# One tuned fp32 kernel: where the first set product is drained, how the z additions are grouped, and a new hand-written order of a unit

## The chip, the core and the metric

The kernel runs on one core of a Trainium2 chip. The metric is device time in microseconds (us) of one execution, the median of several runs; lower is better. Five engines of the core work side by side, each in the order of its own queue: TensorE (PE; its weight loads are listed as PEld), VectorE (DVE), ScalarE (ACT), GpSimd (POOL) and the queue SP, which issues DMAs. Semaphores set who waits for whom.

## What is computed

Attention through 32 packed queries, then a mixture of 8 experts with a balanced gate, then a two-layer network, all in float32:

```python
p_packed = sm_attn(p, k, v)                  # 4 batches, 8 heads, 576 tokens, 64 wide
x = sm_attn(q, p_packed, p_packed)           # reshaped to 2304 tokens x 512
P = exp(x @ w_gate - max), then 8 rounds of row and column scaling
for e in range(8):                           # 512 -> 1024 -> 512
    out += P[:, e:e + 1] * (np.maximum(x @ w1[e], 0.0) @ w2[e])
r = np.maximum(out @ w_in, 0.0)              # 512 -> 2048
result = (s * (r * r) + b) @ w_out           # 2048 -> 512
```

## The kernel before

Products in float32 precision are made from high and low parts: a number is cast to a short form (high), the rest is its low part, and a product is three matmuls (`PASSES`: high x high, high x low, low x high). So every operand needs a cast (ACT) and a subtraction (POOL, or DVE where it comes from PSUM).

The mixture is cut into 32 units (`U1`) of 256 hidden columns. Each unit has four rows, one for each batch b of 576 tokens. Units 5 to 30 run in `slotw` by an order written out by hand, the strings `STEADY[0]` to `STEADY[3]`; unit 4 and the last unit run by `PLAIN`. A string lists tokens, and each token issues the instructions of one step. Each engine keeps that order for its own instructions.

The tokens of a row, for x @ w1 (`mm1w`): seven products m1 to m7 with 288 columns each, a seven-product scheme for a 2 x 2 split. m1 fills bank a; n1 (ACT, L732) copies it into bank b as a seed; m2 adds to b, m6 to a; n2, n3 (ACT, L735) are snapshots of a between m6, m5 and m3; m7 and m4 fill bank e; +b, +c, +e (DVE, L738) add snapshots; rb, rc, ra, re are the ReLU and high part (ACT, L717), lb, lc, la, le the low part (DVE, L721). There are four PSUM banks for these (tag "h").

For h @ w2: t is a tile of 128 tokens x 512 columns, six matmuls (`tile2`, L791), and te its drain by DVE (L813), weighted by the gate, into the sum `acc`. Of each of rows 0, 1 and 2, two tiles are made by seven products p1 to p7 of 256 columns instead (`set7`, L684), one row later, with two of the four "y" PSUM banks, a and b/e. u6, u5, d2, d7, d4, d3 are DVE additions of a bank into `acc` (L690); d3 is put off to the next row's token x. Product 1 belongs to two sums: before, kb (ACT, L702) copies it from bank a into a half of bank b, where p2 adds to it. `bits` and `written` keep which half of a bank has been written. s3 and S (DVE, L646) form sums of h, hs splits them (ACT L666, POOL L667) for p6, p5, p3 and p7 of the next row.

Steps for the unit as a whole: w1a, w1b split W1 (`w1_split`); zh makes z = packed values x W1 (24 matmuls, L555) into all four y banks; zo0, zo1 copy it out (ACT, L565) and send it to DRAM (SP, L567); home brings it back in another layout by four DMAs (SP, L573); za adds (`z_add`, POOL, L587) and zs splits (`z_split`, ACT L594, POOL L595) the left operands of one row; wl loads W2 (SP, L152), w2s splits it, ta adds its quarters (`t_add`, L162) and ts splits the sums (`t_split`); w1l loads the next W1 (SP, L135). hs, cv: one step of the conversion of the last network's weights (from unit 9 on, in each row), which loads and sends by SP (L174, L208). The z tiles share three buffers, the W2, stage and conversion loads two ("raw").

In `steady(u, b)` a step's token belongs to one row: its table is indexed by b. So a step can move within its row alone.

Of the kernel before, what the change touches and what calls it, by code (L numbers as in the profile page):

```python
# [9 lines left out]
F32 = mybir.dt.float32  # L10
# [30 lines left out]
W0 = UE  # L41
# [3 lines left out]
def by7(u, b):  # L45
    return W0 < u < U1 - 1 and b in SEVEN
# [3 lines left out]
def tile_kernel(ctx: ExitStack, tc: tile.TileContext, qT, kT, vv, pb, w1c, w2c, wcat64, wg, sv, bv, out):  # L50
# [107 lines left out]
    def t_add(u):  # L158

        b11, b12, b21, b22 = (raw2[u][:, 256 * n:256 * n + 256] for n in range(4))  # L160
        for to, x_, y_ in ((b11, b12, b11), (b12, b22, b12), (b22, b22, b11), (b21, b21, b22)):
            G.tensor_tensor(out=to, in0=x_, in1=y_, op=ALU.subtract)  # L162
# [19 lines left out]
    def raw_ops(key, q):  # L182

        v, half, f = key
        lo, hi, m = raw_parts(raws[key], q)
        ex = stay[0][:, :256].bitcast(U32) if stay else wt_p[-1].tile([128, 256], U32, tag="ex", name="ex")
        o = slice(512 * half + 256 * q, 512 * half + 256 * q + 256)
# [360 lines left out]
    def z_heads(u):  # L548

        z_ps[:] = [[(psa("y", "ps_z"), written(1))[0] for _ in range(2)] for _ in range(2)]  # L550
# [27 lines left out]
    def z_add(u, b):  # L578

        src = zplain[0][:, b]  # L580
        two = stay[0][:, 256:].rearrange("p (n m) -> p n m", n=2)
        one = wt_p[-1].tile([128, 1, 128], F32, tag="sums", name="sums")
        for to, x_, y_, op in ((two[:, 0], src[:, 0], src[:, 2], ALU.add),
                               (two[:, 1], two[:, 0], src[:, 1], ALU.subtract),
                               (one[:, 0], src[:, 1], src[:, 0], ALU.subtract),
                               (src[:, 0], src[:, 3], two[:, 1], ALU.subtract)):
            G.tensor_tensor(out=to, in0=x_, in1=y_, op=op)  # L587
        z_sums[u, b] = [(slice(0, 4), src), (slice(4, 6), two), (slice(6, 7), one)]

# [79 lines left out]
    def set7(u, b):  # L669
# [34 lines left out]
        jobs = {"p1": p1, "kb": kb, "p7": lambda: product(7, p["e"], True)}  # L704
        for n, to in ((2, "b"), (6, "a"), (5, "a"), (3, "a"), (4, "e")):
# [303 lines left out]
    def slot1(u, pr, q, side=()):  # L1009
# [8 lines left out]
    STEADY = {  # L1018
# [4 lines left out]
    }  # L1023
# [70 lines left out]
    with tc.tile_pool(name="ppf", bufs=1) as ppf_p, tc.tile_pool(name="w1p", bufs=2) as w1_, ExitStack() as whole, ExitStack() as start:  # L1094
# [159 lines left out]
        share(whole, y=4, h=4)  # L1254
        turns["y"] = 0
        wt = whole.enter_context(tc.tile_pool(name="wt", bufs=1))
# [10 lines left out]

        def steady(u, b):

            jobs = ({"zs": (z_split, u, 1), "w1a": (w1_split, u + 1, 0), "w1b": (w1_split, u + 1, 1),  # L1270
                     "za": (z_add, u, 2), "ta": (t_add, u), "ts": (t_split, u)},
                    {"zs": (z_split, u, 2), "zh": (z_heads, u + 1), "zo0": (z_out, 0), "zo1": (z_out, 1),
                     "za": (z_add, u, 3), "zs3": (z_split, u, 3)},
                    {"home": (z_home, u + 1), "wl": (w2_load, u + 1), "za": (z_add, u + 1, 0)},
                    {"zs": (z_split, u + 1, 0), "za": (z_add, u + 1, 1), "w2s": (w2_split, u + 1)})[b]
            if b == 3 and u + 2 < U1:
                jobs["w1l"] = load_w1, u + 2
            if by7(u, b - 1) and b:
                jobs["hs"] = h_split, b - 1
            if u > U1 // 4:  # L1280
                jobs["cv"] = next, units, None
            return jobs

        with tc.manual_schedule():
# [5 lines left out]
                     (1, 2): [(z_add, W0, 0)],  # L1290
                     (1, 3): [(z_split, W0, 0), (z_add, W0, 1)]}
            for u, pr, q in order[cut:]:
                no_gate[:] = [True] * ((pr, q) == (1, 0))
                slot1(u, pr, q, [lambda f=f, a=a: f(*a) for f, *a in first[pr, q]])
            for u in range(W0, U1):
                for b in range(B):
# [20 lines left out]
                    if u == W0:  # L1317
                        if b == 2:
                            at("1", x_split, 3)
                        for place, what in {0: {"1": "w1a", "2": "w1b"}, 1: {"1.5": "zh zo0", "1": "zo1"},  # L1320
                                            2: {"0": "home wl", "3": "za"},
                                            3: {"1.5": "zs", "2": "w1l", "3.5": "za", "4": "w2s"}}[b].items():
                            for token in what.split():
                                at(place, *steady(u, b)[token])
                    elif not last:
                        for token, job in steady(u, b).items():
                            at(token, *job)
                        if u == U1 - 2 and b == 3:
                            at("w2s", plain_home)
                    slotw(u, b, side)  # L1330
# [107 lines left out]
```

## Time and profile before

| | us |
|---|---|
| median of 3 runs | 1715.35 (1714.13 to 1718.73) |
| the profiled execution | 1717.97 |
| its span, first to last instruction | 1716.1 |
| busy in the span: TensorE | 1674.1 (98%) |
| VectorE | 1243.5 (72%) |
| GpSimd | 1137.6 (66%) |
| ScalarE | 981.4 (57%) |

Busy time of matmuls overlaps, since they are pipelined: a 288-column product is shown with some 0.56 us but the next one starts 0.40 us after it. Distances from start to start tell what TensorE spends. A profile's line for an instruction gives its start, its length, its engine and line, output<-inputs, and in brackets the idle time of the engine before it and what ended that.

### The profile page before, as it was taken

To read this page: it belongs to the slowest core of one execution; us is meant where nothing else is said; L and a number is where in the kernel's file an instruction comes from. 1 tells how busy PE (TensorE), PEld (TensorE's weight loads), DVE (VectorE), ACT (ScalarE), POOL (GpSimd) and SP (SyncE) were. 2 spreads that over 40 slices of the span, in tenths; PEclk is the share of its full clock that TensorE was granted. 3 is DMA by queue.
4 is the path that set the end of the run, shared out by engine and by line. 5 is a ranking of instruction groups with operands and counts; after the bars stand their busy time and mean duration, and the time that the engine had idled before them with its cause. 6 is when DMAs were issued, how large, how long until landed. Compare 5 with 4: busy or idle time off the path is not lost.

```text
span 1716.1 us, 29985 instructions
## 1 busy us (share of the span) xinstructions
PE 1674.1 (98%) x10777; PEld 1473.9 (86%) x10777; DVE 1243.5 (72%) x2766; ACT 981.4 (57%) x2320; POOL 1137.6 (66%) x1390
## 2 busy tenths in 40 slices
PE   6999999999999999999999999999999999999999
PEld 4678888888888888888888888888888999999998
DVE  5656656777778777777777778777776878777763
ACT  3443365655665555655565556655655666666664
POOL 0332377888888777888888778888862855555552
PEclk9999999999999999999999999999999999999999
DMA  9610014223232433232233333222320111111102
GB/s 259 172 26 19 7 41 107 75 74 87 74 102 74 103 85 103 74 90 75 77 99 90 88 96 106 75 74 75 91 82 13 37 38 37 50 38 50 39 23 110
DMA packets 62180, 130.39 MB, mean 76 GB/s; under 512 B 5968, under 2 KB 28496, under 8 KB 62032
## 3 DMA queue, kind: packets, MB, share of 16 engines
q1 hardware_dynamic: 62032, 128.49, 27.0%
q8 instruction: 84, 1.38, 0.3%
q14 instruction: 64, 0.52, 0.1%
HBM read 94.39 MB, written 34.08 MB: 75 GB/s over the span
## 4 chain that ended last, share of the span: by engine, by line
PE 62%; ACT 10%; POOL 9%; DMA 9%; DVE 5%; SPq 2%; issue 2%; POOLq 0%; ACTq 0%; DVEq 0%
PE ps L791 31%; PE ps L838 9%; DMA zp<-far 8%; PE ps_a L629 5%; POOL zz L595 5%; ACT zz L594 3%; PE ps_e L629 3%; PE ps L773 2%; PE ps_a L684 2%; PE ps_b L684 2%; SPq L573 2%; PE ps_z L555 2%; ACT stage L565 2%; ACT h L717 2%; POOL ppf L587 2%
## 5 line engine op out<-in xcount | busy, mean ns | idle before, releaser
L791 PE MATMUL ps<-w,h 128*128 128x512 f32 x3360 | 849.8, 394 | 2.1 <-DVE acc L809 0.7
L791 PEld LDWEIGHTS ps<-w,h 128*128 128x128 f32 x3360 | 606.9, 188 | 114.5 <-issue 2.6
L813 DVE SCALAR_TENSOR_TENSOR acc<-ps,pm,acc 128x512 f32<-128x512 f32 x348 | 258.7, 746 | 164.8 <-PE ps L791 164.2
L717 ACT ACTIVATE h<-ps_b 128x288 fp32r<-128x288 f32 x224 | 93.0, 415 | 149.3 <-DVE ps_b L738 70.6
L595 POOL TENSOR_TENSOR zz<-zp,zz 128x512 fp32r<-128x512 f32 x112 | 146.5, 1308 | 41.4 <-ACT zz L594 38.5
L830 POOL TENSOR_TENSOR h<-gt,h 128x384 fp32r<-128x384 f32 x64 | 65.7, 1027 | 120.2 <-ACT h L829 110.8
L735 ACT COPY snap<-ps_a 128x288 f32<-128x288 f32 x232 | 93.5, 403 | 90.3 <-PE ps_a L629 89.2
L629 PE MATMUL ps_a<-xt,zz 128*128 128x288 f32 x672 | 131.6, 304 | 13.2 <-ACT snap L735 12.9
L952 DVE TENSOR_TENSOR acc<-ps,acc 128x512 f32<-128x512 f32 x126 | 86.1, 687 | 80.3 <-PE ps L791 79.9
L629 PEld LDWEIGHTS ps_a<-xt,zz 128*128 128x128 f32 x672 | 103.3, 188 | 34.2 <-ACT snap L735 25.5
L587 POOL TENSOR_TENSOR ppf<-zp 128x128 f32<-128x128 f32 x112 | 51.6, 461 | 113.6 <-DMA zp<-far 113.6
L629 PE MATMUL ps_e<-xt,zz 128*128 128x288 f32 x672 | 126.3, 296 | 0.0
L629 PE MATMUL ps_a<-xa,zz 128*128 128x288 f32 x672 | 126.1, 296 | 0.0
L690 DVE SCALAR_TENSOR_TENSOR acc<-ps_a,pm,acc 128x256 f32<-128x256 f32 x234 | 112.2, 479 | 11.4 <-PE ps_a L684 7.9
L667 POOL TENSOR_TENSOR xa<-hp,xa 128x512 fp32r<-128x512 f32 x78 | 101.1, 1297 | 27.9 <-ACT xa L666 27.9
L721 DVE SCALAR_TENSOR_TENSOR h<-ps_b,h 128x288 fp32r<-128x288 f32 x224 | 100.9, 450 | 24.6 <-ACT h L717 24.5
L690 DVE SCALAR_TENSOR_TENSOR acc<-ps_b,pm,acc 128x256 f32<-128x256 f32 x234 | 109.5, 478 | 5.7 <-PE ps_b L684 5.6
L629 PEld LDWEIGHTS ps_a<-xa,zz 128*128 128x128 f32 x672 | 105.1, 188 | 7.7 <-ACT snap L735 0.3
L838 PE MATMUL ps<-xa,w 128*128 128x384 f32 x432 | 110.4, 336 | 0.0
L838 PE MATMUL ps<-xt,w 128*128 128x384 f32 x432 | 110.1, 335 | 0.0
L629 PEld LDWEIGHTS ps_e<-xt,zz 128*128 128x128 f32 x672 | 104.1, 189 | 4.6
L717 ACT ACTIVATE h<-ps_a 128x288 fp32r<-128x288 f32 x112 | 46.1, 411 | 89.6 <-PE ps_a L629 66.1
(298 smaller groups left out, 3620.0 us busy)
## 6 DMA issues: line engine op xcount, KB each, us to landing
far<-stage SPq DMA_DIRECT2D x54, 512.0 KB, 2.9
zp<-far SPq DMA_DIRECT2D x108, 256.0 KB, 4.6
raw<-w2c SPq DMA_DIRECT2D x32, 512.0 KB, 6.6
raw<-wcat SPq DMA_DIRECT2D x32, 512.0 KB, 3.6
acc<-kT SPq DMA_DIRECT2D x8, 576.0 KB, 9.2
out<-acc SPq DMA_DIRECT2D x18, 256.0 KB, 2.0
acc<-vv SPq DMA_DIRECT2D x5, 576.0 KB, 10.4
conv<-ppf SPq DMA_DIRECT2D x8, 128.0 KB, 4.2
```

What stands on the lines that cost most here:

```text
L587: G.tensor_tensor(out=to, in0=x_, in1=y_, op=op)
L595: G.tensor_tensor(out=zz[:, 1, o], in0=s_, in1=zz[:, 0, o].bitcast(F32), op=ALU.subtract)
L629: mmul(p_[:, :HB], zq_[u, b][:, a, LEFT[n], :], x_, start=start and m == 0, stop=m == 2, skip_group_check=True)
L667: G.tensor_tensor(out=lo, in0=from_, in1=hi.bitcast(F32), op=ALU.subtract)
L690: V.scalar_tensor_tensor(out=a, in0=p[bank], scalar=pm[:, T, e_:e_ + 1], in1=a, op0=ALU.mult, op1=ALU.add)
L717: A.activation(out=h_at(b, f, t)[0], in_=p_[:, :HB], func=AF.Relu)
L721: V.scalar_tensor_tensor(out=hl, in0=p_[:, :HB], scalar=0.0, in1=hh.bitcast(F32), op0=ALU.max, op1=ALU.subtract)
L735: A.copy(s_[n], p["a"][:, :HB])
L791: mmul(y, h[:, f, a, hc:hc + 128], ws[f][k], start=(n == 0), stop=(n == 3 * UF - 1))
L813: V.scalar_tensor_tensor(out=a, in0=y, scalar=pm[:, T, u // UE:u // UE + 1], in1=a, op0=ALU.mult, op1=ALU.add)
L838: mmul(p, w[:, a, c * 128:(c + 1) * 128], x_get(k, c, b), start=(n == 0), stop=(n == 3 * NC - 1))
L952: V.tensor_tensor(out=a, in0=y, in1=a, op=ALU.add)
```

## The change

Product 1 of a set stays in bank a and is added to `acc` by DVE (new token d1) before p6 overwrites it; p2 starts bank b by itself (token p2 takes the bank), and kb, `bits`, `written` and `turns` go.

`z_add(u, b)` adds for rows b and b + 1 in one instruction each: four of 2 x 128 elements in place of eight of 128. It is called for b = 0 and b = 2 (za0, za2). Its sums use all 512 columns of the tile `stay`, so the conversion's scratch tile `ex` moves to a tile of its own. `t_add` makes two of its four subtractions as one.

`steady(u)` is one table for all rows, so that a step can stand in any row of a unit, and all four strings are new: among others, zs3 moves from the end of row 1 to the top of row 2, home and wl swap (wl first) and move to the middle and the end of row 2, za stands in row 2 and row 0 alone, zs0 moves behind p5 of row 3, w2s from row 3 to row 2, zh ahead of n1.

```diff
     def z_add(u, b):
-        src = zplain[0][:, b]
-        two = stay[0][:, 256:].rearrange("p (n m) -> p n m", n=2)
-        one = wt_p[-1].tile([128, 1, 128], F32, tag="sums", name="sums")
+        src = zplain[0][:, b:b + 2]
+        two = stay[0].rearrange("p (b n m) -> p b n m", b=2, n=2)
+        one = wt_p[-1].tile([128, 2, 1, 128], F32, tag="sums", name="sums")
...
-        for to, x_, y_ in ((b11, b12, b11), (b12, b22, b12), (b22, b22, b11), (b21, b21, b22)):
+        for to, x_, y_ in ((left_, up, left_), (b22, b22, b11), (b21, b21, b22)):
...
-        def kb():
-            side = min(bits[turns["y"] % 4])
+        def p2():
             b_ = psa("y", "ps_b2")
-            p["b"], p["e"] = (b_[:, 256 * s:256 * s + 256] for s in (side, 1 - side))
-            written(1 - side)
-            A.copy(p["b"], p["a"])
+            p["b"], p["e"] = b_[:, :256], b_[:, 256:]
+            product(2, p["b"], True)
...
-        for k, t, d, bank in (("u6", 1, 0, "a"), ("u5", 1, 1, "a"), ("d2", 0, 0, "b"), ("d7", 1, 1, "e"),
+        for k, t, d, bank in (("d1", 0, 0, "a"), ("u6", 1, 0, "a"), ("u5", 1, 1, "a"), ("d2", 0, 0, "b"), ("d7", 1, 1, "e"),
...
     STEADY = {
-        0: "m1 m7 zs n1 ta t te m2 m6 rb n2 t m5 x lb t w1a n3 m3 te +c s3 S m4 w1b te +e ra cv rc t ts za t te te x lc re le la",
-        1: "m1 x n1 zh zo0 m6 zo1 hs m2 n2 p1 t m7 kb rb p2 te p6 zs p7 lb u6 m5 d2 p5 n3 t +c m4 u5 s3 d7 te rc +e m3 ra p3 d3 re lc le za p4 zs3 la S cv d4",
-        2: "m1 n1 x p1 t m2 m6 rb n2 m7 t home m5 hs kb te te lb p2 p6 cv u6 n3 p7 +c t d7 rc p5 m3 d2 lc m4 u5 ra za +e s3 p4 p3 S d4 re le wl d3 te la",
-        3: "m1 n1 p1 m2 x m6 hs zs rb n2 t kb m5 lb p6 te m7 p2 u6 n3 p7 +c p5 m4 d2 rc t lc za w2s +e d7 m3 u5 te re p4 ra d4 le p3 d3 w1l cv la",
+        0: "m1 n1 t m2 ta m6 w1a x t rb lb n2 te te zs1 m5 cv w1b t te x t m7 n3 +c ts te s3 t m4 m3 rc za2 te +e ra lc re le S la",
+        1: "m1 zh n1 m6 cv m7 m2 zo0 hs n2 p1 zo1 m5 rb n3 x t lb p2 d1 +c zs2 p6 p7 rc m4 u6 d2 d7 m3 p5 +e t p4 te u5 ra s3 re p3 le d4 d3 lc S te la",
+        2: "zs3 m7 t m1 n1 te t m6 hs te n2 p1 m2 rb m5 n3 x wl d1 p2 w2s p6 lb p7 +c m3 m4 u6 d7 +e p5 s3 t u5 re rc ra p3 home p4 d3 S la lc za0 d4 te le d2",
+        3: "m1 cv m7 p1 n1 x m6 m2 hs d1 n2 end p2 m5 n3 t rb lb p6 p7 cv m3 +c m4 u6 d7 p5 +e zs0 re ra u5 p4 d4 rc te le t p3 w1l d2 te d3 lc la",
     }
```

## Rows read from the trace of the kernel before

**Rows 1.** The page's busy line of the whole span: busy us, share, instructions.

```profile
PE 1674.1 (98%) x10777; PEld 1473.9 (86%) x10777; DVE 1243.5 (72%) x2766; ACT 981.4 (57%) x2320; POOL 1137.6 (66%) x1390
```

**Rows 2.** Windows: length, busy by engine, clock: stretch, two units, a piece.

```profile
239.46:1239.02 999.56, 981.89 (x6278) 875.63 (x6277) 762.52 (x1765) 589.28 (x1477) 796.93 (x1010) 1.00 0.32 87
...
469.25:507.29 38.04, 37.72 (x245) 33.75 (x244) 29.52 (x70) 22.67 (x57) 30.92 (x40) 1.00 0.32 87
...
584.87:626.07 41.20, 39.26 (x245) 35.29 (x244) 30.06 (x70) 22.66 (x57) 30.77 (x40) 0.96 0.35 90
...
610.07:613.48 3.41, 3.41 (x18) 3.41 (x17) 1.91 (x5) 1.74 (x3) 3.21 (x7) 0.53 0.00 0
```

**Rows 3.** Waits of weight loads, 239.46 to 1239.02: us in total, times, longest.

```profile
PEld ps_a L629 <- ACT snap L735: 23.7, 26, 2.2
PEld ps_b L629 <- ACT ps_b L732: 9.0, 26, 1.0
```

**Rows 4.** Timeline of TensorE in row 3 of one unit: start, length, instruction.

```profile
488.89 0.52 PE L684 MATMUL ps_a<-w,h 128*128 128x256 f32 x3
489.52 0.66 PE L629 MATMUL ps_b<-xa,zz 128*128 128x288 f32 x3
...
490.42 1.53 PE L791 MATMUL ps<-w,h 128*128 128x512 f32 x6
492.16 0.67 PE L629 MATMUL ps_a<-xt,zz 128*128 128x288 f32 x3 [0.20 <-ACT snap L735]
...
494.87 1.54 PE L791 MATMUL ps<-w,h 128*128 128x512 f32 x6
496.25 0.56 PE L629 MATMUL ps_a<-xa,zz 128*128 128x288 f32 x3
496.65 0.52 PE L684 MATMUL ps_b<-w_t,h 128*128 128x256 f32 x3
497.01 0.51 PE L684 MATMUL ps_a<-w,xa 128*128 128x256 f32 x3
```

**Rows 5.** Timeline of ACT in the same row.

```profile
489.08 0.38 ACT L732 COPY ps_b<-ps_a 128x288 f32<-128x288 f32 x1 [0.20 <-PE ps_a L629]
...
490.38 0.63 ACT L594 CAST zz<-zp 128x512 fp32r<-128x512 f32 x1 [0.38 <-POOL zp L587]
...
491.72 0.38 ACT L735 COPY snap<-ps_a 128x288 f32<-128x288 f32 x1
```

**Rows 6.** Timeline of POOL in the same row.

```profile
488.39 0.46 POOL L587 TENSOR_TENSOR ppf<-zp 128x128 f32<-128x128 f32 x1 [3.95 <-DMA zp<-far]
...
490.31 1.30 POOL L667 TENSOR_TENSOR xa<-hp,xa 128x512 fp32r<-128x512 f32 x1
```

**Rows 7.** Groups by line and shape: count, busy us, mean ns, idle before.

```profile
L690 DVE SCALAR_TENSOR_TENSOR acc<-ps_a,pm,acc 128x256 f32<-128x256 f32 x234 | 112.2, 479 | 11.4 <-PE ps_a L684 7.9
...
L293 POOL TENSOR_TENSOR w<-raw,w 128x1024 fp32r<-128x1024 f32 x28 | 67.6, 2414 | 0.7 <-ACT w L292 0.7
...
L587 POOL TENSOR_TENSOR sums<-zp 128x128 f32<-128x128 f32 x112 | 51.6, 461 | 0.0
...
L702 ACT COPY ps_b<-ps_a 128x256 f32<-128x256 f32 x78 | 31.0, 398 | 0.0
```

**Rows 8.** Timeline of DVE in the same row 3.

```profile
490.02 0.74 DVE L813 SCALAR_TENSOR_TENSOR acc<-ps,pm,acc 128x512 f32<-128x512 f32 x1
490.67 0.45 DVE L721 SCALAR_TENSOR_TENSOR h<-ps_a,h 128x288 fp32r<-128x288 f32 x1
491.04 0.48 DVE L690 SCALAR_TENSOR_TENSOR acc<-ps_a,pm,acc 128x256 f32<-128x256 f32 x1
```

**Rows 9.** Timeline of SP, the DMA issues ahead of that row.

```profile
481.26 1.74 SPq L573 DMA_DIRECT2D zp<-far  x4
483.05 0.44 SPq L152 DMA_DIRECT2D raw<-w2c  x1
```

**Rows 10.** The page's DMA issues: count, KB each, us to landing.

```profile
far<-stage SPq DMA_DIRECT2D x54, 512.0 KB, 2.9
```

More of the change, by code (lines that the diff above doesn't have):

```diff
@@ L158, in t_add @@
     def t_add(u):
-        b11, b12, b21, b22 = (raw2[u][:, 256 * n:256 * n + 256] for n in range(4))
-        for to, x_, y_ in ((b11, b12, b11), (b12, b22, b12), (b22, b22, b11), (b21, b21, b22)):
+        r = raw2[u].rearrange("p (k n) -> p k n", k=2)
+        b11, b12, b21, b22 = (r[:, k, 256 * n:256 * n + 256] for k in range(2) for n in range(2))
+        up = bass.AP(b12.tensor, b12.offset, [b12.ap[0], [512, 2], [1, 256]])
+        left_ = r[:, 0].rearrange("p (k n) -> p k n", k=2)
+        for to, x_, y_ in ((left_, up, left_), (b22, b22, b11), (b21, b21, b22)):
             G.tensor_tensor(out=to, in0=x_, in1=y_, op=ALU.subtract)
@@ L185, in raw_ops @@
         lo, hi, m = raw_parts(raws[key], q)
-        ex = stay[0][:, :256].bitcast(U32) if stay else wt_p[-1].tile([128, 256], U32, tag="ex", name="ex")
+        ex = wt_p[-1].tile([128, 256], U32, tag="ex", name="ex")
         o = slice(512 * half + 256 * q, 512 * half + 256 * q + 256)
@@ L548, in z_heads @@
     def z_heads(u):
-        z_ps[:] = [[(psa("y", "ps_z"), written(1))[0] for _ in range(2)] for _ in range(2)]
+        z_ps[:] = [[psa("y", "ps_z") for _ in range(2)] for _ in range(2)]
         for c in range(NC):
@@ L578, in z_add @@
     def z_add(u, b):
-        src = zplain[0][:, b]
-        two = stay[0][:, 256:].rearrange("p (n m) -> p n m", n=2)
-        one = wt_p[-1].tile([128, 1, 128], F32, tag="sums", name="sums")
[L583 to L586, printed above, removed]
+        src = zplain[0][:, b:b + 2]
+        two = stay[0].rearrange("p (b n m) -> p b n m", b=2, n=2)
+        one = wt_p[-1].tile([128, 2, 1, 128], F32, tag="sums", name="sums")
+        for to, x_, y_, op in ((two[:, :, 0], src[:, :, 0], src[:, :, 2], ALU.add),
+                               (two[:, :, 1], two[:, :, 0], src[:, :, 1], ALU.subtract),
+                               (one[:, :, 0], src[:, :, 1], src[:, :, 0], ALU.subtract),
+                               (src[:, :, 0], src[:, :, 3], two[:, :, 1], ALU.subtract)):
             G.tensor_tensor(out=to, in0=x_, in1=y_, op=op)
-        z_sums[u, b] = [(slice(0, 4), src), (slice(4, 6), two), (slice(6, 7), one)]
+        for i in range(2):
+            z_sums[u, b + i] = [(slice(0, 4), src[:, i]), (slice(4, 6), two[:, i]), (slice(6, 7), one[:, i])]
     def z_split(u, b):
@@ L1266, in tile_kernel, with steady @@
         units = conv_units()
[L1268 to L1276, printed above, removed]
+        def steady(u):
+            jobs = {"zs1": (z_split, u, 1), "w1a": (w1_split, u + 1, 0), "w1b": (w1_split, u + 1, 1),
+                    "za2": (z_add, u, 2), "ta": (t_add, u), "ts": (t_split, u), "zs2": (z_split, u, 2),
+                    "zh": (z_heads, u + 1), "zo0": (z_out, 0), "zo1": (z_out, 1), "zs3": (z_split, u, 3),
+                    "home": (z_home, u + 1), "wl": (w2_load, u + 1), "za0": (z_add, u + 1, 0),
+                    "zs0": (z_split, u + 1, 0), "w2s": (w2_split, u + 1)}
+            if u + 2 < U1:
                 jobs["w1l"] = load_w1, u + 2
-            if by7(u, b - 1) and b:
-                jobs["hs"] = h_split, b - 1
             if u > U1 // 4:
@@ L1320, in tile_kernel @@
                         for place, what in {0: {"1": "w1a", "2": "w1b"}, 1: {"1.5": "zh zo0", "1": "zo1"},
-                                            2: {"0": "home wl", "3": "za"},
-                                            3: {"1.5": "zs", "2": "w1l", "3.5": "za", "4": "w2s"}}[b].items():
+                                            2: {"0": "home wl", "3": "za0"},
+                                            3: {"1.5": "zs0", "2": "w1l", "4": "w2s"}}[b].items():
                             for token in what.split():
-                                at(place, *steady(u, b)[token])
+                                at(place, *steady(u)[token])
                     elif not last:
-                        for token, job in steady(u, b).items():
+                        for token, job in steady(u).items():
                             at(token, *job)
+                        if by7(u, b - 1) and b:
+                            at("hs", h_split, b - 1)
                         if u == U1 - 2 and b == 3:
-                            at("w2s", plain_home)
+                            at("end", plain_home)
                     slotw(u, b, side)
```

16 lines of the change are left out of this document (4 added, 12 removed).

## The prediction

> **What bounds the kernel now.** I read the page's busy line first [rows 1]: TensorE 98%, the other engines 57 to 72%. So TensorE paces the kernel, and a change that leaves its matmuls alone can only win back time in which TensorE stands. This change leaves them alone: seven 288-column products a row, seven 256-column products in three rows of four, twelve 512-column tiles and one head product a unit, before and after. The question is thus how long TensorE stands in the stretch whose order is rewritten, and what the new order makes of that.
>
> The windows by stretch [rows 2] give its length: from the head product of one unit to that of the next, 26 times, 999.56 us, a mean of 38.44 us. A common unit takes 38.04 us, a bad one 41.20 us. So 26 x (38.44 - 38.04) = 10.4 us of the stretch lie in bad units, the rest in something that every unit has.
>
> The waits of the weight loads name that something [rows 3]: 26 waits for a snapshot copy of ACT (L735) and 26 for the copy that seeds bank b (L732), one of each in a unit; what else TensorE waits for there is a few us. Their place is seen in TensorE's timeline of row 3 [rows 4]. In undisturbed places a 288-column product takes 0.40 us from start to start, a 256-column one 0.36, a tile 1.38. Product 1 of the second set starts at 488.89, so m2 should start at 489.25; it starts at 489.52, 0.27 us late: the seed runs on ACT from 489.08 to 489.46 [rows 5] and only 0.36 us of work stands between m1 and m2. The tile at 490.42 should end at 491.80, m5 starts at 492.16, 0.36 us late. It waits for a snapshot that ACT began at 491.72, and ACT was late because the casts of the next unit's z (490.38) stand ahead of it in its queue and waited for POOL's z additions, which waited 3.95 us for the four DMAs that bring z home [rows 5, 6]. The first matmul after each stop takes about 0.1 us more (the products at 489.52 and 492.16 last 0.66 and 0.67 us, against about 0.5 to 0.56 elsewhere). Together 0.27 + 0.36 + 0.2 = 0.83 us a unit, 21.6 us in 26 units. The bad units are the same place with the homecoming later: in the one of 41.20 us the granted clock fell to 0.53 for 3.41 us after that wait [rows 2].
>
> So the pool of gain is 21.6 + 10.4 = 32 us, and a unit without these stops would take 38.04 - 0.83 = 37.2 us.
>
> **The change, part by part.** *Set product 1 drained by DVE.* Out go 78 ACT copies of 0.398 us (31.0 us of ACT), in come 78 DVE additions of 0.479 us (37.4 us, 1.44 us a unit) [rows 7]. Both engines have idle time: DVE is busy 29.5 of 38.04 us in a unit, ACT 22.7 [rows 2]. Directly it costs nothing while the addition ends before p6 overwrites its bank; without that cover it costs up to 0.48 us a row. p2 starts its own bank and waits for no copy.
>
> *z additions for two rows.* Eight POOL instructions of 0.461 us [rows 7] become four of 256 elements. No row has that addition; between 128 elements (0.461) and 512 (1.30, two-dimensional like these [rows 6]) a line gives 0.74, and the bounds are 0.461 and 2 x 0.461. At 0.74, POOL saves 16 x 0.461 - 8 x 0.74 = 1.5 us a unit (bounds 0 and 3.7). But the group that follows the homecoming grows: from 1.92 us (488.39 to 490.31 [rows 6]) to about 2.9 (bounds 1.9 and 3.7), and row 3's split of the second set's left operands stands behind it on POOL. In the additions of `t_add` one 512-element operation takes the place of two of 256: 1.30 against 1.48, nothing, as POOL idles about 7 us in a unit.
>
> *The order.* I set the new rows out with the three durations of [rows 4] and ask at each place where TensorE needs another engine how much TensorE work stands between. A snapshot or seed needs 0.63 us from the start of the product behind its source (488.89 to 489.52), if ACT is free.
>
> Row 0: a tile stands behind m1 and behind m6, over 1.3 us each. Row 1: the head product (1.6 us) stands behind m1; behind m6 stand m7, m2, p1 (1.16 us), and ACT owes two stage copies and a cast first, which I count out to end about 0.1 us early. Row 2: a tile behind m1; p1 and m2 (0.76) behind m6. Row 3: m7 and p1 (0.76) behind m1, m2 and p2 (0.76) behind m6. So both places of row 3 that stop now are cleared, m5's above all because zs0 now stands behind n3 and rb on ACT: a late homecoming no longer holds a snapshot. Three places are left with 0.1 us in hand.
>
> p6 needs d1, p5 needs u6, p4 needs d7, p3 needs u5, m4 needs +c, all DVE. At starts of about 0.65 us for a tile's drain and 0.37 for a low part [rows 8], 0.48 at most for a set's addition, DVE carries about 30.9 of 37.2 us. It is tightest from the end of row 2 into row 3: d4, te, le, d2 and a conversion step are still to come when row 3 starts, and I find la and lc (which free the banks of m7 and n1) and d1 done 0.2 to 0.5 us before TensorE asks. Bound: no stop, or half a us a unit.
>
> The homecoming: SP issues its four DMAs when POOL's last split of the old z is done, 1.74 us for the four, and POOL starts on it 7.1 us after the first issue (481.26 to 488.39) [rows 6, 9]. zs3 moves from the end of row 1 to the top of row 2, but its casts wait for nothing of row 2: on ACT they follow re of row 1, done about 1.2 us before that row ends. The first cast takes 0.6 us, the three splits of 512, 256 and 128 elements 1.3 + 0.74 + 0.46 = 2.5, so POOL ends about 1.9 us into row 2 and z is home 9.0 us into it. The w2s cast follows n3 on ACT and ends some 6.7 us into the row, POOL's split of it (2.41 us [rows 7]) at 9.1; then the additions (2.9) to 12.0, then hs's low part (1.3) to 13.3. Row 2 is 9.46 us long, and p6 of row 3 starts 4.1 us into the row, its third matmul 0.24 later: 13.8. So 0.5 us in hand. A homecoming over 0.5 us late costs its excess, against all of it now.
>
> SP's queue: the load of W2 (wl) now stands ahead of the homecoming, before it stood behind (483.05) [rows 9]. It needs its raw buffer, which in the units with conversions is freed when the second stage write has landed. That one is issued in the middle of row 1, at about 4.6 us, and takes 2.9 us [rows 10], to 7.5; the homecoming is due 1.9 us into row 2, at 11.7, some 4 us later. w2s comes up on ACT about 8 us after that, and finds its data. The conversions' loads and sends, the stage copies and w1l keep their places among the DMAs to within a row.
>
> At this spot the Trainium skill speaks against the change: "DMA: Bandwidth & Descriptors", section Queues, rings and completion order, says that an engine's descriptors are consumed in ring order, so 512 KB put ahead of the homecoming go first. The trace agrees as far as it goes: the four 256 KB reads issued within 1.74 us are waited for 7.1 us. By that rule alone, with both due at once, the kernel gets slower; that is the third rival.
>
> **The sum.** Pool 32 us. Against it: five places with 0.1 to 0.2 us in hand, put at 0.15 us a unit together, 4 us; of the bad units' 10.4 us about 4 stay (each homecoming that is over 0.5 us late). Edges (the units before and after, where the additions are paired too): nothing. Gain 32 - 8 = 24 us. The profiled execution took 1717.97 us (span 1716.1 and 1.9 around it), so 1694; the median of the runs shown is 1715.35, 2.6 lower, so 1691 on that.
>
> **Rivals.** (1) DVE or ACT is late at the narrow places: half a us a unit instead of 0.15, 9 us less gain, 1700 to 1704. For it: 83% of DVE and margins of 0.1 to 0.5 that rest on starts read in one row; against it: each is positive. (2) The homecoming now holds p6: if additions and w2s put hs 0.9 us later than worked out, 26 x 0.9 = 23 us, the whole gain, 1714. For it: the longer additions; against it: both inputs come from rows of the same unit. (3) The other side: wl goes out right ahead of the homecoming. Its 512 KB are two of the steps of [rows 9]; (7.1 - 1.74) / 4 = 1.3 us each as a price, 2.6 us later home, 2.1 us of stop behind p6 in each unit. A wait that long also drops the clock, as [rows 2] show, for up to another 1.5 us in some units. 26 x 2.1 = 55 less 24: slower by about 30, 1745. It decides when wl leaves SP over 4 us later than worked out above, or anything else makes the homecoming over 1.5 us late. (4) The stops only move, and the change does not do what an order is for: 1715.
>
> **How the numbers follow.** Forecast, gain of 16 to 33 us (1682 to 1699): 0.65. Rival 1, 0.14. Rivals 2 and 4, 0.12, nine tenths of it within 5.1 us of before. Rival 3 and worse, 0.07; 0.02 for a gain over 33 us. A change of 0.3% (5.1 us) is about what a measurement of this kernel can tell from none. Faster 0.82, same 0.11, slower 0.07. The range 1681 to 1710 takes in the forecast and rival 1.
>
> **What would show it.** Right: units of about 37.3 us from head product to head product; the loads' waits for L735 and L732 in the stretch down from 32.7 to under 10 us; ACT's copy at L702 gone, 78 more DVE additions at the set's line; half as many z additions of 0.70 to 0.80 us. Wrong: a wait of the set's products for POOL's xa in row 3 (rival 2, or with 2 us each rival 3), of m4, p3 to p6 or m7 for DVE (rival 1). The prediction falls if the homecoming is issued later than about 2.5 us into row 2.

## The result, and the profile after

The changed kernel takes 1691.02 us (median of 4 runs, 1690.33 to 1693.49), the kernel before on the same chip 1714.74 (1711.99 to 1718.73): a ratio of 0.9862, with an interval of 0.984 to 0.9885. The forecast was 1691.0. The profiled execution took 1690.33 us, 27.6 less than that of before. Of the spans' difference, 27.5 us, the stretch of [rows 2] gives 24.0 us, the part ahead of it 2.5 and the part behind it 1.0. The 2.5 can't be laid to the change: the first head product comes anywhere from 236.5 to 241.8 us in the fourteen traces of this case, at 236.9 in one whose additions are not paired (e1) and at 241.8 in one whose are (e10).

The page after, its span, its busy line, the shares of the chain that ended last, and the set's additions:

```profile
span 1688.6 us, 29741 instructions
...
PE 1660.2 (98%) x10777; PEld 1471.4 (87%) x10777; DVE 1254.3 (74%) x2844; ACT 950.9 (56%) x2242; POOL 1100.5 (65%) x1140
...
PE 93%; DVE 2%; POOL 2%; ACT 2%; issue 1%; DMA 0%; SPq 0%; POOLq 0%; ACTq 0%; DVEq 0%
...
L686 DVE SCALAR_TENSOR_TENSOR acc<-ps_a,pm,acc 128x256 f32<-128x256 f32 x312 | 144.2, 476 | 14.5 <-PE ps_a L680 14.1
```

TensorE's share of busy time is 98%, as in [rows 1], and would have told nothing: a matmul that starts late behind a wait of 0.3 us hardly shows in a share of 1,700 us. The chain tells it. Before, as the page before has it, 62% of it was TensorE; now 93% is:

```profile
PE 62%; ACT 10%; POOL 9%; DMA 9%; DVE 5%; SPq 2%; issue 2%; POOLq 0%; ACTq 0%; DVEq 0%
```

The set's additions went from 234 [rows 7] to 312 at the same length, and ACT has 78 instructions fewer.

The windows (length, busy by engine, clock, as in [rows 2]): the stretch, its first two units, a common unit. Each runs from one head product to the next; the cuts, here as in [rows 2], lie 0.24 us ahead of the head product's first matmul. The head product stands in row 1, so the first window is mostly unit 4, which runs by `PLAIN` (203 matmul records, where a unit has 245), and the second mostly unit 5, the first by the new order.

```profile
236.91:1212.48 975.57, 970.69 (x6278) 874.76 (x6277) 771.53 (x1837) 559.54 (x1401) 764.22 (x778) 1.00 0.33 89
...
236.91:276.44 39.53, 36.59 (x203) 30.53 (x202) 22.10 (x42) 21.61 (x51) 22.76 (x25) 1.00 0.29 80
276.44:316.29 39.85, 37.91 (x245) 33.88 (x244) 29.21 (x70) 21.56 (x55) 33.17 (x34) 1.00 0.31 80
...
465.62:502.95 37.33, 37.33 (x245) 33.77 (x244) 29.97 (x73) 21.52 (x55) 29.73 (x32) 1.00 0.33 89
```

The stretch takes 975.57 us where [rows 2] had 999.56. Of its 26 windows all but the first two take 37.33 us or very near it (37.54 at most). There is no bad unit any more.

The waits of the weight loads in that stretch (total us, times, longest), the counterpart of [rows 3]:

```profile
PEld ps_e L625 <- DVE h L714: 4.5, 25, 0.2
PEld ps_z L550 <- issue: 4.2, 26, 0.2
PEld ps_a L680 <- POOL xa L663: 1.8, 1, 1.8
PEld ps L784 <- ACT stage L560: 1.5, 1, 1.5
PEld ps_a L625 <- ACT snap L728: 1.4, 1, 1.4
```

Both stops of [rows 3] are gone: the snapshot (now L728) has one wait of 1.4 us, the seed (now L725) none. In their place stands a small one, m7's bank (L714), 0.2 us a unit. The three single waits below it lie in the first two windows.

TensorE at the end of row 2 and in row 3 of the unit of 465.62, to be laid beside [rows 4] (row 3 starts with the product at 484.65):

```profile
475.21 0.56 PE L625 MATMUL ps_e<-xt,zz 128*128 128x288 f32 x3
...
484.65 0.56 PE L625 MATMUL ps_a<-xa,zz 128*128 128x288 f32 x3
485.15 0.66 PE L625 MATMUL ps_e<-xt,zz 128*128 128x288 f32 x3
...
486.01 0.66 PE L625 MATMUL ps_a<-xt,zz 128*128 128x288 f32 x3
486.51 0.56 PE L625 MATMUL ps_b<-xa,zz 128*128 128x288 f32 x3
486.91 0.51 PE L680 MATMUL ps_b<-w,h 128*128 128x256 f32 x3
487.26 0.57 PE L625 MATMUL ps_a<-xt,zz 128*128 128x288 f32 x3
...
489.04 0.52 PE L680 MATMUL ps_a<-w_t,xa 128*128 128x256 f32 x3
```

m5 (487.26) now starts 0.35 us behind p2, as a 256-column product lets it, and m2 (486.51) waits for no seed. What is left of loss lies at the top: m7 (485.15) starts 0.1 us late, and m7 and m6 (486.01) take 0.66 us in place of 0.56, as a first matmul behind a wait does, so that the next product comes 0.50 us behind each in place of 0.40. m7 needs bank a of the row ahead, which la frees on DVE (484.65), and m6 the seed, which needs bank b, freed by lc (485.01):

```profile
484.65 0.45 DVE L714 SCALAR_TENSOR_TENSOR h<-ps_a,h 128x288 fp32r<-128x288 f32 x1
485.01 0.45 DVE L714 SCALAR_TENSOR_TENSOR h<-ps_b,h 128x288 fp32r<-128x288 f32 x1
```

The homecoming and what follows it, on SP and POOL of the same unit (before: [rows 6, 9]; row 2 starts at 475.21):

```profile
472.50 0.33 SPq L144 DMA_DIRECT2D raw<-w2c  x1
475.82 1.74 SPq L568 DMA_DIRECT2D zp<-far  x4
```

```profile
474.50 1.30 POOL L591 TENSOR_TENSOR zz<-zp,zz 128x512 fp32r<-128x512 f32 x1 [1.10 <-ACT zz L590]
475.75 0.74 POOL L591 TENSOR_TENSOR zz<-ppf,zz 128x256 fp32r<-128x256 f32 x1
...
481.94 2.41 POOL L288 TENSOR_TENSOR w<-raw,w 128x1024 fp32r<-128x1024 f32 x1 [2.01 <-ACT w L287]
484.29 0.76 POOL L582 TENSOR_TENSOR ppf<-zp 128x256 f32<-128x256 f32 x1
...
487.34 1.48 POOL L663 TENSOR_TENSOR xa<-hp,xa 128x512 fp32r<-128x512 f32 x1
```

The reads leave as soon as POOL's split of 512 columns is over (474.50 + 1.30 = 475.80); they do not wait for the split at 475.75, which reads another tile. No wait for a DMA stands ahead of the additions at 484.29, where [rows 6] had 3.95 us: what lets them start is the end of the w2s split ahead of them. The last read lands at 482.91, 17.05 us behind the head product's first matmul (465.86), so the data lies ready 1.4 us before POOL turns to it. The paired additions take 0.74 to 0.76 us each. hs ends at 488.82; p6's third matmul, the first to need it, comes 0.24 us behind 489.04.

### The profile page after: what moved, and what is told of

Same layout as the page of the kernel before. It is cut to its first block, busy times and chain, and to the rows that moved or that the text cites. A ratio compares the mean times of both kernels' runs of the same rounds, so it can differ in the third digit from the quotient of the medians.

```text
span 1688.6 us, 29741 instructions
## 1 busy us (share of the span) xinstructions
PE 1660.2 (98%) x10777; PEld 1471.4 (87%) x10777; DVE 1254.3 (74%) x2844; ACT 950.9 (56%) x2242; POOL 1100.5 (65%) x1140
## 3 DMA queue, kind: packets, MB, share of 16 engines
q1 hardware_dynamic: 62032, 128.49, 27.6%
## 4 chain that ended last, share of the span: by engine, by line
PE 93%; DVE 2%; POOL 2%; ACT 2%; issue 1%; DMA 0%; SPq 0%; POOLq 0%; ACTq 0%; DVEq 0%
PE ps L784 44%; PE ps_a L625 11%; PE ps L831 9%; PE ps_a L680 7%; PE ps_e L625 5%; PE ps_b L680 5%; PE ps_b L625 3%; PE ps_z L550 2%; PE ps L766 2%; PE ps_a L901 1%; PE ps_e L901 1%; PE ps_z L496 0%; PE ps_f L953 0%; PE ps_v L375 0%; PE ps_t L365 0%
## 5 line engine op out<-in xcount | busy, mean ns | idle before, releaser
L714 DVE SCALAR_TENSOR_TENSOR h<-ps_b,h 128x288 fp32r<-128x288 f32 x224 | 101.4, 453 | 89.3 <-ACT h L710 88.0
L686 DVE SCALAR_TENSOR_TENSOR acc<-ps_a,pm,acc 128x256 f32<-128x256 f32 x312 | 144.2, 476 | 14.5 <-PE ps_a L680 14.1
L728 ACT COPY snap<-ps_a 128x288 f32<-128x288 f32 x232 | 94.2, 406 | 57.5 <-PE ps_a L625 56.1
L625 PE MATMUL ps_a<-xa,zz 128*128 128x288 f32 x672 | 121.8, 295 | 2.0 <-ACT snap L728 1.0
L725 ACT COPY ps_b<-ps_a 128x288 f32<-128x288 f32 x104 | 39.9, 383 | 148.9 <-PE ps_a L625 99.2
L625 PEld LDWEIGHTS ps_a<-xa,zz 128*128 128x128 f32 x672 | 101.0, 189 | 5.9 <-ACT snap L728 1.4
L288 POOL TENSOR_TENSOR w<-raw,w 128x1024 fp32r<-128x1024 f32 x28 | 67.4, 2406 | 54.9 <-ACT w L287 50.9
```

The lines of the kernel that those rows point to most:

```text
L625: mmul(p_[:, :HB], zq_[u, b][:, a, LEFT[n], :], x_, start=start and m == 0, stop=m == 2, skip_group_check=True)
L686: V.scalar_tensor_tensor(out=a, in0=p[bank], scalar=pm[:, T, e_:e_ + 1], in1=a, op0=ALU.mult, op1=ALU.add)
L714: V.scalar_tensor_tensor(out=hl, in0=p_[:, :HB], scalar=0.0, in1=hh.bitcast(F32), op0=ALU.max, op1=ALU.subtract)
L728: A.copy(s_[n], p["a"][:, :HB])
```

## The experiments

The theory was that the whole gain is two stops of row 3 and the late homecomings behind them, and that it comes from the order; the first rival, that one part alone carries it (kb's copy off ACT, the pairs off POOL, or the one step zs moved behind the snapshots). Each ratio below is against runs of the kernel before on the same chip.

**Product 1 drained by DVE, old order** (`e1_d1_alone`): kb becomes d1 in the three old strings, and p2 starts its own bank, as in the change.

```diff
-        1: "... m2 n2 p1 t m7 kb rb p2 ..."
+        1: "... m2 n2 p1 t m7 d1 rb p2 ..."
-        2: "... home m5 hs kb te te ..."
+        2: "... home m5 hs d1 te te ..."
-        3: "... rb n2 t kb m5 lb p6 ..."
+        3: "... rb n2 t d1 m5 lb p6 ..."
```

> The old order with one part of the change: product 1 drained by DVE (d1 stands where kb stood), p2 starting its own bank. Theory (the gain is the order's): both stops of row 3 stay, since neither waits for kb; units of 38.0 us, 1711 to 1719, ratio 0.998 to 1.002. Rival (the copy on ACT was a good part of what held the snapshots): the waits for L735 fall by a third, 1707 or less.

1715.7 us, ratio 1.000 (0.9987 to 1.0012). Both stops stand as in [rows 3] (lines shifted by two; a few us fall to the window):

```profile
PEld ps_a L629 <- ACT snap L733: 25.3, 26, 2.1
PEld ps_b L629 <- ACT ps_b L730: 9.0, 26, 1.0
```

31 us of ACT's work changed engine and nothing moved: in the old order ACT was late for what stood ahead of the snapshot in its queue, not for the amount of its work.

**The paired additions alone, old order** (`e2_pairs_alone`), with the scratch tile that goes with them; of the edit, the lines that say the most:

```diff
-        src = zplain[0][:, b]
+        src = zplain[0][:, b:b + 2]
...
-        1: "... rc re lc le za p4 zs3 la S cv d4"
+        1: "... rc re lc le p4 zs3 la S cv d4"
-        3: "... rc t lc za w2s +e ..."
+        3: "... rc t lc w2s +e ..."
```

> The old order with the z additions for two rows at once (and the scratch tile of the conversion that goes with it). Theory: the group behind the homecoming takes 2.9 to 3.05 instead of 1.92 us and the casts that hold the snapshot of row 3 wait for it, so m5 stops about 1.1 us more in each unit: 26 x 1.1 = 28, and a lower clock after the long waits of the bad units, 1740 to 1760. Rival (POOL's saved 1.5 us a unit is what counts): 1715 or less.

1769.17 us, ratio 1.0313 (1.028 to 1.0347), worse than I expected. Most units take 39.8 to 40.2 us, five take 41.8 to 44.05. Its waits, and the window of one of the five (columns as in [rows 2]):

```profile
PEld ps_a L630 <- ACT snap L736: 49.4, 25, 3.2
PEld ps_a L685 <- POOL xa L668: 18.2, 24, 2.2
```

```profile
602.20:646.09 43.89, 40.70 (x245) 36.35 (x244) 30.07 (x70) 22.78 (x57) 29.34 (x32) 0.92 0.33 85
```

m5's stop grew from 0.36 to about 1.5 us, as four additions of 0.74 ahead of the cast make it (2.96 against 1.92 us). What I had not expected is the second line: in row 0 the pair also stands right ahead of row 1's hs, and p6 of row 1 waits for that, 0.69 us in most units. In the unit shown the stop is 3.0 us, and its mean clock falls to 0.92.

**The casts moved behind the snapshots, old order** (`e3_casts_behind`): one token.

```diff
-        3: "... x m6 hs zs rb n2 t kb m5 lb p6 te m7 p2 u6 n3 p7 ..."
+        3: "... x m6 hs rb n2 t kb m5 lb p6 te m7 p2 u6 n3 zs p7 ..."
```

> The old kernel with one token moved: zs in row 3 from ahead of n2 to behind n3. Theory: the stop of m5 goes (0.36 + 0.1 us a unit, 12 us) and with it most of the bad units' 10.4 us, the stop of m2 stays: 1691 to 1702, about 1696. Rival (a new wait takes its place, because the casts now come later for the next row, or p6 meets POOL's part of hs): 1710 or more.

1734.6 us, ratio 1.0111 (1.0087 to 1.0135). Here my theory fell: taking the cause of m5's stop away in the old order costs 19 us. The waits in the stretch, and POOL in row 3 of one unit and in row 1 of the next, whose window is cut at 512.00:

```profile
PEld ps_b L629 <- ACT ps_b L732: 18.7, 48, 1.0
PEld ps_a L684 <- POOL xa L667: 14.8, 29, 1.1
PEld ps_b L684 <- ACT ps_b L702: 13.8, 19, 0.8
```

```profile
498.29 1.30 POOL L595 TENSOR_TENSOR zz<-zp,zz 128x512 fp32r<-128x512 f32 x1 [1.81 <-ACT zz L594]
...
517.45 1.28 POOL L667 TENSOR_TENSOR xa<-hp,xa 128x512 fp32r<-128x512 f32 x1
```

m5's stop is gone, and two others have come, about 1.1 us a unit together at p6 and p2 of the next row 1, beside a second wait for the seed. POOL now waits 1.81 us for the late casts at 498.29, and then never pauses again until hs at 517.45, 5.45 us behind that cut. In the kernel before, the same hs starts 4.11 us behind its cut at 507.29, and from 491.57 on POOL pauses only twice ahead of it:

```profile
506.71 2.39 POOL L293 TENSOR_TENSOR w_t<-raw,w_t 128x1024 fp32r<-128x1024 f32 x1 [0.24 <-ACT w_t L292]
...
511.40 1.30 POOL L667 TENSOR_TENSOR xa<-hp,xa 128x512 fp32r<-128x512 f32 x1 [0.38 <-ACT xa L666]
```

So the old order has a second limit close behind the first: from row 3 to hs of the next row 1 POOL has 0.6 us of slack, and a cast that is 1.8 us later pushes hs into p6. ACT, over the same time, shows that the waits of the seed and of p2 come from POOL as well:

```profile
502.68 0.62 ACT L594 CAST zz<-zp 128x512 fp32r<-128x512 f32 x1 [0.99 <-POOL zp L587]
...
515.60 1.08 ACT L565 COPY stage<-ps_z 128x512 f32<-128x512 f32 x2 [1.06 <-POOL w_t L293]
```

Row 0's casts (502.68) wait 0.99 us for z additions that POOL makes late behind its pause, and the seed stands behind them; kb, for which p2 waits, stands behind a stage copy (515.60) that waits 1.06 us for POOL's split of w_t.

**All three, old order** (`e4_three_parts`): the edits of e1, e2 and e3 together.

```diff
-        3: "... x m6 hs zs rb n2 t kb m5 lb p6 te m7 p2 u6 n3 p7 +c p5 m4 d2 rc t lc za w2s +e ..."
+        3: "... x m6 hs rb n2 t d1 m5 lb p6 te m7 p2 u6 n3 zs p7 +c p5 m4 d2 rc t lc w2s +e ..."
```

> The old order with d1, the paired additions and the moved casts together. Theory: the casts no longer hold the snapshot, but the longer additions put POOL's part of hs about 1.0 us later, to about 0.2 us behind the third matmul of p6: 0.3 us a unit and the bad units in full, 1700 to 1712, so worse than the moved casts alone. Rival (the parts add up): 1690 to 1696, at or below the moved casts alone.

1737.38 us, ratio 1.0123 (1.0095 to 1.0151). p6 waits for POOL in row 1 and in row 3:

```profile
PEld ps_a L685 <- POOL xa L668: 37.7, 49, 2.2
```

So the parts together, without the order, lose 1.2%, and with it they gain 1.4%: the order is what turns them. The new order without either part was not run, and the merged subtractions of `t_add` are neither in this run nor undone in any. Beside the pairs the casts' move has the other sign than in e3: this run, with d1 besides, is 32 us faster than e2.

**How far POOL's queue explains e3** (`e12_casts_behind_w1_dve`): e3 with the low parts of W1 (four subtractions a unit) made by DVE, to give POOL slack ahead of row 1's hs.

```diff
-        split(w1s[u][:, :, o], wts[1, u][:, o])
+        split(w1s[u][:, :, o], wts[1, u][:, o], V)
```

> The old kernel with the moved casts (zs of row 3 behind n3, 1735 us) and, besides, the low parts of w1a and w1b made by DVE instead of POOL: 2.55 us a unit less in POOL's queue, in the place where that run shows POOL without a pause from row 3 to hs of the next row 1. Theory (the moved casts only shift the stop because POOL's queue has no slack, and hs and p6 of row 1 meet the delay): the stop of row 1 goes, units of 37.4 to 37.8 us, 1696 to 1708. Rival (the delay in row 1 comes from elsewhere, ACT's copies kb and n1): units of 38.8 us or more, 1725 or more. DVE's two additional operations may cost up to 0.3 us a unit.

1722.54 us, ratio 1.0043 (1.0026 to 1.006): 12 us better than e3, still 7 over before, between what the two theories expected.

```profile
PEld ps_b L629 <- ACT ps_b L732: 18.8, 48, 1.0
PEld ps_a L684 <- POOL xa L667: 10.0, 27, 0.9
PEld ps_b L684 <- ACT ps_b L702: 4.7, 13, 0.6
```

p6's wait for POOL fell from 14.8 to 10.0 us and p2's for kb's copy from 13.8 to 4.7; those for the seed did not move. POOL's new slack was partly spent waiting for ACT's cast of w_t, 1.16 us at 507.69. So relief of POOL gives back 12 of the 19 us, a large part of what e3 ran into. The seed's second wait, some 10 us in e3 as here, stands behind the casts of row 0 shown there, which wait for POOL ahead of the place of w1a and w1b, so the relief comes too late for it. The edit also loads DVE, and what the rest of p6's wait hangs on I have not separated: that much of e3 stays open.

**The order with its casts put back ahead** (`e5_casts_ahead`): the changed kernel, zs0 ahead of n2.

```diff
-        3: "... x m6 m2 hs d1 n2 end p2 ... p5 +e zs0 re ra u5 ..."
+        3: "... x m6 m2 hs zs0 d1 n2 end p2 ... p5 +e re ra u5 ..."
```

> The changed kernel with one token put back: zs0 in row 3 ahead of n2, as before. Theory: the snapshot n2 waits on ACT behind casts that wait for POOL's additions, which end at about the time m5 is due; m5 stops 1.65 + 0.1 us a unit, 26 x 1.75 = 45 us: 1730 to 1765 with some lower clock. Rival (homecoming early enough that this place no longer matters): 1691 to 1700.

1737.11 us, ratio 1.0134 (1.0119 to 1.0149), 46 us over the changed kernel. The units take 39.03 us, and the stop of [rows 3] is back, larger, as in e2, where the additions ahead of the cast are paired too:

```profile
PEld ps_a L625 <- ACT snap L728: 41.4, 25, 1.7
```

Of the steps that a run undoes, this is the one on which the gain hangs most; the others of the new order (home and wl, zs3, w2s, zh, the products of row 3) were not undone one by one. e3 and e5 belong together: much the same move costs 19 us in the old order and is worth 46 in the new one.

**The order without pairs** (`e6_unpaired`): eight additions of 128 in place of four of 256, at the same places.

```diff
+        for i in range(2):
...
-            G.tensor_tensor(out=to, in0=x_, in1=y_, op=op)
+            G.tensor_tensor(out=to[:, i], in0=x_[:, i], in1=y_[:, i], op=op)
```

> The changed kernel with the z additions of a pair of rows made as eight instructions of 128 elements again, in the same place. Theory: the group behind the homecoming takes 3.85 instead of 3.05 us, hs's low part ends 0.8 us later, 0.35 us behind the third matmul of p6 in row 3: 0.45 us a unit, 12 us, 1703 (1696 to 1708). Rival (there is more room than the trace shows): 1691. Rival (the pairing is a main part of the gain): over 1710.

1702.32 us, ratio 0.9933 (0.9918 to 0.9948). p6 of row 3 waits for POOL in each unit, 0.25 to 0.54 us (the 2.6 is the single wait in the second window):

```profile
PEld ps_a L681 <- POOL xa L664: 12.0, 25, 2.6
```

Eight at a distance of about 0.48 us take 0.8 us more than the four (484.29 to 487.34 above); 0.45 of it was room, the rest reaches TensorE. The pairs are worth 11 us here, and lose 53 in the old order.

**kb put back in the new order** (`e10_kb_back`): the ACT copy and the banks of before, kb ahead of p2.

```diff
-        3: "m1 cv m7 p1 n1 x m6 m2 hs d1 n2 end p2 m5 ..."
+        3: "m1 cv m7 p1 n1 x m6 m2 hs kb n2 end p2 m5 ..."
```

> The changed kernel with the first part undone: product 1 is copied by ACT (kb) into bank b again and p2 adds to it, no d1; kb stands ahead of p2 in row 1, ahead of rb in row 2 and ahead of n2 in row 3. Theory (the order, not the drain, carries the gain): n2 of row 3 ends 0.3 us later, still before m5, and DVE is 1.4 us a unit lighter: 1686 to 1696. Rival (the drain by DVE is what lets the new order work): p2 or m5 stops 0.3 us or more in each of three rows, 1700 or more.

1697.77 us, ratio 0.9902 (0.9886 to 0.9918): between the two expectations. Units take 37.57 us, 0.24 more, and the wait is p2's in row 3:

```profile
PEld ps_b L688 <- ACT ps_b L706: 4.4, 25, 0.2
```

So d1 is worth some 6 us in the new order (6.75 by the medians, 5.8 by the stretch), and nothing in the old one (e1). Its use is not that it takes work from ACT but that p2 waits for no copy where row 3 is dense.

**A later homecoming, first try** (`e7_late_home`): a load of 512 KB that nothing uses, issued ahead of the four reads.

```diff
         zp_new()
+        more = far_p.tile([128, 1024], F32, tag="more", name="more")
+        nc.sync.dma_start(out=more, in_=w2c[u])
         for c in range(NC):
```

> The changed kernel with one more 512 KB transfer (W2 of the unit, from DRAM to a DRAM tile that nobody reads) put on SP right ahead of the homecoming. It comes home 2.5 us or more later. By the margin of the prediction (0.5 us) p6 of row 3 stops 2.0 + 0.1 us a unit or more: 1745. By the margin of the changed kernel's trace (home at 482.67, needed at 484.3 plus 0.45 us: 2.1 us) p6 stops 0.4 + 0.1 us: 1704, and more by 26 us for each us that the transfer holds the homecoming beyond 2.5 us. Home's landing and p6's stop are read from the same run.

1692.15 us, ratio 0.9876 (0.9861 to 0.9891): as good as nothing. The extra load does not wait for the z buffer, so SP issued it 4.8 to 8.3 us behind the head product's first matmul, before the reads, whose last one landed 16.9 to 19.1 us behind it (17.9 on average) in place of 16.9 to 17.8 (17.2), the first two windows left out. In two of these units, with landings at 18.82 and 19.07, p6 of row 3 waited for POOL, 0.26 and 0.19 us; in the others not at all.

**A later homecoming, second try** (`e9_late_home_mid`): the same load between the first and the second of the four reads, where it cannot leave early.

```diff
         for c in range(NC):
...
+            if c == 0:
+                more = far_p.tile([128, 1024], F32, tag="more", name="more")
+                nc.sync.dma_start(out=more, in_=w2c[u])
```

> The changed kernel with one more 512 KB transfer (W2, from DRAM to a DRAM tile that nobody reads) between the first and the second of the four transfers that bring z home, so that it can't go out early as it did ahead of all four. Three of the four come home some 2.5 to 3 us later than 17.05 us behind the head product. By the prediction's margin of 0.5 us p6 of row 3 stops 2.0 to 2.5 us a unit (52 to 65 us, 1745 to 1760). By the margin in the changed kernel's trace, 2.1 us, it stops 0.4 to 0.9 us and 0.1 for the restart (13 to 26 us, 1704 to 1717). Landing and stop are read from the same run; their difference is the margin.

1708.82 us, ratio 0.9964 (0.995 to 0.9978). SP in one unit (head product's first matmul at 509.63), and POOL at the homecoming:

```profile
519.60 0.32 SPq L568 DMA_DIRECT2D zp<-far  x1
519.96 0.75 SPq L572 DMA_DIRECT2D more<-w2c  x1
520.76 1.54 SPq L568 DMA_DIRECT2D zp<-far  x3
```

```profile
529.57 0.74 POOL L585 TENSOR_TENSOR ppf<-zp 128x256 f32<-128x256 f32 x1 [1.45 <-DMA zp<-far]
```

Over the units of the new order the last read lands 2.0 us later, 19.2 us behind the head product's first matmul on average (18.4 to 20.4). Landing (us behind that matmul) and the stop of p6 in five units:

| last read lands | p6 stands |
|---|---|
| 18.48 | 0 |
| 19.10 | 0.30 |
| 19.42 | 0.54 |
| 19.55 | 0.66 |
| 19.78 | 0.93 |

The stop begins at about 18.85; units that land at 18.9 to 19.0 still show none that the profile lists, and one at 18.87 shows 0.26, so this holds to some 0.2 us. The usual landing is at 17.05, so the homecoming has 1.8 us in hand, not 0.5.

At this point the Trainium skill's rule of the third rival, "DMA: Bandwidth & Descriptors", section Queues, rings and completion order (descriptors are consumed in ring order), is seen on both sides. This trace agrees where the 512 KB are due with the reads: 2.0 us later, against the 2.6 us that I had estimated from [rows 6, 9]. Where the load leaves earlier, the same place ahead in the queue costs little: from the first read's issue to the last landing the median is 7.0 us before, 7.1 in the changed kernel, where W2's load leaves ahead, 7.8 in e7 and 9.1 in e9.

**The narrow place at the top of row 3** (`e8_lc_first`): lc ahead of S and la at the end of row 2.

```diff
-        2: "... p3 home p4 d3 S la lc za0 d4 te le d2"
+        2: "... p3 home p4 d3 lc S la za0 d4 te le d2"
```

> The changed kernel with one swap in row 2: lc ahead of S and la on DVE. Theory: what is left of stops in a unit is m7 of row 3 waiting for a bank that la frees and the seed n1 behind lc; with lc first, m7 gets bank b's place 0.6 us sooner and n1 the one of la, 0.3 us sooner: units of 37.0 instead of 37.33 us, 26 x 0.3 = 8 us, 1683. Rival (S later makes hs and so p6 late): 1691 or more.

1684.2 us, ratio 0.9825 (0.9808 to 0.9841): faster than the changed kernel's 1691.02, and than the kernel before. The intervals of the two ratios just touch; the length of the units settles it. A unit, and the longest waits of the weight loads in the stretch:

```profile
465.57:502.64 37.07, 37.07 (x246) 33.74 (x245) 30.21 (x74) 21.52 (x55) 29.71 (x31) 1.00 0.34 90
```

```profile
PEld ps_z L550 <- issue: 4.2, 26, 0.2
PEld ps_a L680 <- POOL xa L663: 1.8, 1, 1.8
```

m7's wait is gone, and with it m6's: 26 x (37.33 - 37.07) = 6.8 us, which is what the medians show. lc needs only rc, which ACT ends before ra; it now fills the pause of 0.50 us in which DVE stood in front of S, waiting for ra. Counted from the head product, S and la start some 0.07 us later than in the changed kernel, lc 1.4 us sooner and the seed 0.33 us sooner; m7 no longer waits for la.

**The first units** (`e11_w2s_sooner`): e8 with unit 4's w2s one place sooner, against the 1.8 us of p6 in the first unit that follows it.

```diff
-                                            3: {"1.5": "zs0", "2": "w1l", "4": "w2s"}
+                                            3: {"1.5": "zs0", "1": "w2s", "2": "w1l"}
```

> The changed kernel with lc ahead of S and la in row 2, and w2s of the unit before the stretch one place sooner in its row 3. Theory: units of 37.07 us as with the first edit alone, and the stop of p6 in the first unit of the stretch (1.77 us, behind POOL's part of hs) gone or halved, 1681 to 1684. Rival (that stop has another cause): 1684.

1684.65 us, ratio 0.982 (0.9805 to 0.9834): no gain over e8. p6's stop is gone; in the window ahead the loads' wait for a snapshot has grown from 1.4 to 2.4 us.

## Why the prediction was right, and where its steps were not

**What bounds the kernel: right.** The distances of [rows 4] and the pool of 32 us are what the runs showed. A unit was forecast at 37.3 us and takes 37.33. In the stretch, the common unit's 38.04 - 37.33 = 0.71 us make 18.5 us (forecast 17.6), the bad units 10.4 (forecast 6.4), and the first two windows give 5 us back (forecast nothing): 24 of 24.

**That the stops would go and not move: right, but the reason was thinner than it read.** "zs0 now stands behind n3 and rb on ACT" was given as what clears m5. e5 shows that it does, e3 that by itself it only makes room for the next limit, POOL's row 3 to row 1, which I hadn't listed: the prediction looked at what needs TensorE in the new order and was right there, and named no second bound of the old one. It didn't have to, since the whole order was new; for a prediction of e3 it failed.

**The set's product 1: right in sign.** "Directly it costs nothing" holds (e1). That p2 waits for no copy was in the working, but without a price; it is worth some 6 us.

**The pairs: right.** 0.74 us each, as the line between the two lengths gave. hs was forecast to end 0.5 us ahead of need; it ends 0.45 ahead. That room is what e6 uses up.

**The homecoming: the mis-sized term.** I had SP's first read 1.9 us into row 2 and z home 9.0 us into it. The reads leave at 475.82, 0.6 us into the row, and land 7.7 us into it. The step that failed is "when POOL's last split of the old z is done": I counted all three splits (1.3 + 0.74 + 0.46), and only the first of them reads the z tile; the other two are the 1.2 us that were too much. The w2s split was forecast to end 9.1 us into the row, and does (484.35). So it, and not the homecoming, opens the additions, and a late homecoming has 1.8 us in hand (e9) where I gave it 0.5. That is why none of the bad units stayed, where I let 4 us of them stay: before, behind the first window, the last read lands at 18.7 to 19.1 us in the units of up to 38.4 us and at 19.4 to 20.3 in the six of 38.7 to 41.2, and even the latest, 1.5 us over the usual, would fit into 1.8; in the changed kernel, behind the first two windows, the latest is 0.7 us over the usual.

**Edges: wrong.** "Nothing" was measured as 5 us lost in the first two windows (39.53 and 39.85 us). About 2 us of them are the price of unit 4's paired additions: the first window takes 37.4 to 38.0 us in the five traces without pairs, e6 among them, and 39.5 or more in the nine with them. The waits there for ACT's stage copy and snapshot, 1.5 and 1.4 us, are 0.5 and 0.3 in e6. The second window's stop of 1.8 us at p6 stands before too, with 1.1 us. The two errors in the stretch, 4 us too little for the homecoming and 5 too much at the edges, nearly cancelled; that the sum came out so much better than its terms is luck.

**The narrow places: forecast 0.15 us a unit, measured 0.26** (after less e8), and both at the place that was named, the end of row 2 into row 3 on DVE. That e8's 37.07 lies below the 37.2 us that I gave for a unit without any of these stops says that before had some 0.1 us more of small losses than I listed; I have not traced them.

**The rivals.** The first (DVE late at narrow places) happened in small. The second (hs holds p6) is what e6 shows, at half of its price (11 us of 23). The third (wl ahead of home) didn't decide: wl leaves 3.3 us ahead of the reads (472.50 against 475.82), close to the 4 us worked out, and the 2.0 us of delay that e9 measures would for the most part have gone into the 1.8 us in hand.

## What to carry to other kernels

Where one engine paces the kernel, find its stops by the distances from start to start, and for each stop the queue in which the releaser stood behind something late; taking work off that engine did nothing here while the order of its queue stayed (e1). A step that is moved out of one wait arrives later for everybody behind it: look up how much the next engine pauses up to its own next deadline (0.6 us here) before calling the move free (e3). Parts that lose one by one can be needed together, so undo each of them in the finished kernel as well as adding each to the old one.

## What the runs showed of the hardware that I had not expected

POOL and DVE slow each other on operands in SBUF. In the changed kernel, 18 of the 78 subtractions of hs on POOL take 1.34, 1.35 or 1.48 us, the other 60 about 1.29. Each of the 18, and none of the 60, runs beside one of DVE's conversion steps, whose operands all lie in SBUF (L183 to L194); operations of DVE that read PSUM run beside the 60 without such a mark. In the stretch before, no hs meets such a step, and none takes over 1.31 us. DVE pays too: a step with one input takes 0.28 us where POOL is idle for part of it, and 0.34 to 0.45 where POOL runs throughout; one with two inputs 0.41, and 0.47 to 0.57. In e8 the step that overlaps hs starts 0.3 us earlier, on the last z addition, and takes 0.66 and 0.79 us. In the unit shown this took 0.19 us of the room in front of p6 (1.48 in place of 1.29). The Trainium skill names such a thing ("GPSIMD Engine Reference", section 1. Specifications: the SBUF interfaces are shared with VectorE, with contention where the DVE instruction has two SBUF inputs or runs in a two-port mode), and this trace agrees for the steps with two inputs; whether those with one input ran in such a mode, it does not show. The working of the 0.5 us had left the contention out.
